# Moving half of attention's K projection into the w2 stage as a seven-product scheme

## The chip, the cores and the metric

The kernel runs on one core of one Trainium2 chip. The metric is device time in microseconds (us). A time of a kernel is the median of its runs, with the lowest and the highest in brackets. "Span" is the time from the first to the last instruction of the one execution that was profiled; it is some 2 us shorter than the device time of the same kernel (654.1 us against a median of 655.91 before).

The engines are called PE or TensorE (matmul), VectorE (DVE in the profile), ScalarE (ACT), GpSimd (POOL) and SyncE (SP, which issues nearly all DMAs here: 266 of 267 in the kernel before).

## The reference

One layernorm of x feeds two branches, whose results are added to x: a token-mixing MLP (B) and an attention with a memory over four segments (A). Only what bears on the change:

```python
# x: 2048 tokens x 1024, bf16; 32 heads of 32; N = 4 segments of L = 512 tokens
q = (xn @ wq)...; k = (xn @ wk)...; v = (xn @ wv)...      # split in heads and segments
phi = lambda t: where(t > 0, t + 1, exp(t))
M, z = 0, 0
for s in range(N):
    p = softmax(qs @ ks.T * scale + mask)                 # within the segment
    a_dot = p @ vs
    a_mem = (phi(qs) @ M) / (phi(qs) @ z + 1e-6)          # from the segments before
    outs.append(g * a_mem + (1 - g) * a_dot)
    M, z = M + phi(ks).T @ vs, z + sum(phi(ks))
attention = concat(outs) @ wo
mlp = w2.T-product of gelu(w1-product of layernorm(xn))   # over tokens; 3584 hidden
result = x + attention + mlp
```

phi(K) of the last segment is never used, so it is needed for three segments only.

## The kernel before

Three stages follow one another: w1 pairs, w2 pairs, attention.

**The seven-product stages.** A pair of output column blocks is computed as a product of 2x2 blocks with seven instead of eight block products. VectorE makes the sums of the weight blocks and the differences of the activation blocks, PE makes the seven products in a fixed order, and the results are put together while they leave PSUM. A w2 pair has 7 x 14 = 98 matmuls of 128x128 by 128x512, so 14 matmuls to a product.

```python
ORDER = (1, 6, 5, 7, 2, 4, 3)
order += [(i, p) for i in range(2, n1 + self.N_W2) for p in self.ORDER]
for i, p in order:
    ...
    self.product(pair, p)                                # PE: `depth` matmuls into one bank
    (self.after1 if i < n1 else self.after2)(pair, p)    # VectorE, ScalarE, GpSimd, DMA

def add_bank(self, pair, acc, dst, src):                 # on VectorE, "part" in the profile
    ... tensor_tensor(self.tmp[dst][:], self.bank(b), self.tmp[src][:], op=ALU.add)

def after2(self, pair, p):
    ...
    elif p == 4:
        finish("Y", 1, 0, t1); self.put_out(...)         # store to DRAM
        if i + 2 < self.N_W2:
            self.load_w2(i + 2)                          # 1.8 MB
    ...
    if i == self.N_W2 - 1:
        self.before_attention(p)                         # at p == 2: loads wo, 2 MB
```

**Attention.** It runs in 32 units, eight groups of four heads in each of four segments. Between the logits and the weighted sums, dense jobs of eight matmuls (projections q, k, v and the output product wo) fill PE. A dense job takes bank 6 or 7 in turn, and so it waits until the job before last has been copied out of that bank: K on VectorE (`kT`), q on ScalarE. In the views below, `ost` are a unit's weighted sums copied out of PSUM, `prod` and `o_s` its scaled and added output, `oT` the transpose of that, and `fin` the rows of the result.

```python
STOPS, STOPS_DVE = (1, 4, 7), (1, 4)

def dense(self, n, side=True):                # n matmuls of the waiting jobs
    while n > 0 and self.jobs:
        ...                                   # bank 6 or 7 in turn
        elif self.side and stop in stops:
            self.side.popleft()()             # hand one item of side work to VectorE here

def unit_jobs(self, u):
    jobs = [self.wo_job(*x) for x in self.wo_plan.get(u, ())]
    if m < 2 * N_SEG: jobs.append(self.v_job(m, u % 4))
    if u + 2 < N_UNIT: jobs += [self.q_job(u + 2), self.k_job(u + 2)]
    return jobs

def attention(self):
    ...                      # wo jobs of segment 2 in units [27, 28, 29, 30, 30, 31, 31, 31]
    self.load_fin(0); self.load_fin(1)
    for u in range(N_UNIT):
        even = u % 2 == 0
        if u in self.XN_AT[::4]:
            self.xn_load(xn); self.xn_load(xn + 1)        # x for the next segment: "xs"
        if u < 10:
            cuts = self.cut(total, (0, 4, 2, 4, 1, 13, 8) if even else (7, 3, 2, 4, 1, 15))
        else:
            cuts = self.cut(total, (0, 4, 2, 2, 2, 14, 8) if even else (7, 3, 2, 2, 2, 16))
        self.dense(cuts[0]); self.logits(u, 0)            # logits, then a 128x2048 exp on ScalarE
        self.dense(cuts[1], end); ...; self.weigh(u - 1, 0)
        ...
        if N_GRP <= u: self.side.append(lambda u=u: self.phi_q(u))
        if u + 1 < N_UNIT: self.side.append(lambda u=u: (self.phi_k(u + 1), self.k_transpose(u + 1)))
        if xn is not None: self.side.append(lambda c=xn: (self.xn_scale(c), self.xn_transpose(c), ...))
        self.dense(cuts[4]); self.logits(u, 1)
        if even: self.dense(cuts[5]); self.logits(u, 2)   # this exp serves both units of the pair
        self.dense(100)
```

Two units share five big exps (three in the even, two in the odd one). So the time from the first exp of an even unit to the first exp of the next even unit is the time of a pair of units, and I read all of attention by these starts.

The softmax here doesn't subtract the row's maximum and nothing guards it: scores larger than these inputs give would overflow.

## Time and profile before

Time before: 655.91 us (655.87 to 655.92, four runs).

| what | value | read from |
|---|---|---|
| span | 654.1 us | page |
| PE busy | 98% of the span | page, busy table |
| chain of waits | 92% on matmuls | page, chain |
| w2 stage up to the first big exp | 182 to 363.8 us | stretches, exps |
| pair of units with 48 dense matmuls (units 2 to 7) | 15.02 us | starts of exps |
| pair of units with 64 (units 12, 14, 20, 22) | 18.93 us | starts of exps |
| from unit 30's first exp to the end | 31.6 us | starts of exps, span |

First the page of the kernel before: busy time by engine, then the shares of the chain of waits by engine.

```profile
span 654.1 us, 11050 instructions
...
PE 642.6 (98%) x4572; PEld 303.4 (46%) x4627; DVE 422.5 (65%) x797; ACT 276.1 (42%) x297; POOL 152.9 (23%) x181
...
PE 92%; DVE 4%; issue 1%; DMA 1%; ACT 1%; SPq 0%; DVEq 0%
```

PE is the bound: nearly the whole span can be followed back through matmuls. The next view, of the same kernel, is busy time in stretches of the span. Its columns are the stretch, its length, the busy time of PE, weight loads, VectorE, ScalarE and GpSimd (with instruction counts), the granted PE clock, the DMA share and GB/s.

```profile
182.00:349.00 167.00, 167.00 (x775) 75.61 (x774) 70.34 (x89) 6.44 (x11) 34.17 (x29) 1.00 0.59 157
363.80:438.00 74.20, 72.26 (x787) 36.01 (x800) 50.57 (x120) 59.76 (x50) 27.37 (x40) 1.00 0.73 156
607.20:654.10 46.90, 43.15 (x444) 22.30 (x451) 35.38 (x68) 21.95 (x16) 14.46 (x16) 1.00 0.39 105
```

The w2 stage has room everywhere but on PE: VectorE works 70 of 167 us, ScalarE 6. That invites the change. The last two units are another matter. The timeline of ScalarE in the kernel before (start, duration, line, tiles, and in brackets the idle time before with its releaser) shows exps of which the last three begin 2.38 us apart, although each takes 1.88:

```profile
622.46 1.88 ACT L1216 ACTIVATE pT<-ps_all 128x2048 bf16<-128x2048 f32 x1 [0.66 <-PE ps_all L198]
...
625.22 1.88 ACT L1216 ACTIVATE pT<-ps_all 128x2048 bf16<-128x2048 f32 x1 [0.36 <-PE ps_all L198]
627.60 1.88 ACT L1216 ACTIVATE pT<-ps_all 128x2048 bf16<-128x2048 f32 x1 [0.50 <-PE ps_all L198]
629.98 1.88 ACT L1216 ACTIVATE pT<-ps_all 128x2048 bf16<-128x2048 f32 x1 [0.50 <-PE ps_all L198]
```

The exp needs the logits, and the logits need the banks that the exp before has read. In none of the profiled runs do two of these exps begin closer than 2.37 us, so I take this round trip of about 2.38 us as a floor, an estimate from these starts.

### The profile page before, as it was taken

Reading aid. Unit: us, or ns where it says so; the run is one execution under the profiler, and the core shown is the slowest. Engines: PE = TensorE matmul, PEld = TensorE weight load, DVE = VectorE, ACT = ScalarE, POOL = GpSimd, SP = SyncE. Lnnn points to the kernel's source line nnn. Section 1 sums busy time; section 2 is a strip of 40 time slices with the busy share of each in tenths; the row PEclk is TensorE's granted clock in tenths of the full one; section 3 lists DMA queues with packets and bytes.
Section 4 is the critical chain, followed back from the end, with each engine's and each line's share of the span. In section 5 each row is a group of like instructions: output and inputs, shape, how many; then the busy total and the mean of one; then the engine's idle time right before and its main releaser. Section 6 shows DMA issues by size and latency. Waiting matters only on the chain.

```text
span 654.1 us, 11050 instructions
## 1 busy us (share of the span) xinstructions
PE 642.6 (98%) x4572; PEld 303.4 (46%) x4627; DVE 422.5 (65%) x797; ACT 276.1 (42%) x297; POOL 152.9 (23%) x181
## 2 busy tenths in 40 slices
PE   8999999999999999999999999999999999999998
PEld 3444444444444444444444445554554455454444
DVE  6885775665644553355422376688889988867795
ACT  6642232232210000000011677886766777667760
POOL 2410000000010222022210234343243324323450
DMA  9804242242557546854386587865547754544325
GB/s 301 215 0 130 65 114 80 65 124 69 144 162 189 150 123 165 194 144 115 96 225 201 138 171 144 170 146 114 130 114 177 146 128 92 121 113 82 83 81 137
DMA packets 187258, 87.65 MB, mean 134 GB/s; under 512 B 116040, under 2 KB 174408, under 8 KB 187208
## 3 DMA queue, kind: packets, MB, share of 16 engines
q1 hardware_dynamic: 187064, 86.91, 53.0%
q8 instruction: 36, 0.59, 0.4%
q14 instruction: 14, 0.11, 0.0%
q10 hardware_dynamic: 144, 0.03, 0.0%
HBM read 67.13 MB, written 8.39 MB: 115 GB/s over the span
## 4 chain that ended last, share of the span: by engine, by line
PE 92%; DVE 4%; issue 1%; DMA 1%; ACT 1%; SPq 0%; DVEq 0%
PE ps_all L198 92%; DMA w1early<-in_B_w_dram 1%; ACT pT L1216 1%; DVE fin L1448 1%; DVE prod L1313 1%; DVE ost L1267 1%; DVE mtmp L1080 0%; DVE mtmp L1082 0%; SPq L220 0%; DVE fin L1158 0%; DVE kT L1112 0%; DVE xs L986 0%; DVE srec L1309 0%; DVE MZbf L1277 0%; DVE pqT L1082 0%
## 5 line engine op out<-in xcount | busy, mean ns | idle before, releaser
L1216 ACT ACTIVATE pT<-ps_all 128x2048 bf16<-128x2048 f32 x80 | 150.1, 1876 | 55.6 <-PE ps_all L198 55.6
L1220 POOL TENSOR_SCALAR_AFFINE_SELECT pT<-pT 128x512 bf16<-128x512 bf16 x128 | 104.1, 831 | 189.0 <-ACT pT L1216 188.8
L690 DVE TENSOR_TENSOR part<-ps_all,part 128x512 f32<-128x512 f32 x76 | 52.5, 691 | 118.9 <-PE ps_all L198 118.1
L926 POOL TENSOR_TENSOR part<-part,stg 128x512 f32<-128x512 f32 x24 | 33.0, 1404 | 263.5 <-DVE part L690 263.5
L695 ACT ACTIVATE part<-ps_all 128x512 f32<-128x512 f32 x20 | 11.9, 597 | 149.0 <-PE ps_all L198 149.0
L742 ACT ACTIVATE g<-part,b1c 128x512 f16<-128x512 f32 x36 | 26.0, 722 | 98.8 <-DVE part L690 98.8
L198 PE MATMUL ps_all<-wv,xnT 128*128 128x512 bf16 x238 | 64.6, 379 | 1.8 <-issue 0.6
L198 PE MATMUL ps_all<-wo,oT 128*128 128x512 bf16 (+2 forms) x254 | 61.0, 366 | 1.1 <-issue 0.6
L198 PE MATMUL ps_all<-xnT,wq 128*128 128x512 bf16 x248 | 61.2, 380 | 0.2
L198 PE MATMUL ps_all<-xnT,wk 128*128 128x512 bf16 x245 | 59.6, 379 | 1.5 <-issue 1.4
L1267 DVE CAST ost<-ps_all 128x396 bf16<-128x396 f32 (+2 forms) x96 | 44.5, 475 | 23.8 <-PE ps_all L198 22.3
L198 PEld LDWEIGHTS ps_all<-vA,pT 128*128 128x128 bf16 x1280 | 45.6, 96 | 20.3 <-DVE ost L1267 3.5
L198 PE MATMUL ps_all<-g,w2s 128*128 128x512 f16 x224 | 51.0, 379 | 0.0
L198 PE MATMUL ps_all<-g,sum 128*128 128x512 f16 x224 | 51.0, 379 | 0.0
L198 PE MATMUL ps_all<-gT,sum 128*128 128x512 f16 x224 | 49.7, 379 | 0.0
L198 PE MATMUL ps_all<-vA,pT 128*128 128x33 bf16 x1280 | 48.5, 177 | 0.7 <-DVE ost L1267 0.5
L198 PE MATMUL ps_all<-h,sum 128*128 128x512 f16 x192 | 45.2, 379 | 0.0
L198 PE MATMUL ps_all<-h,w1s 128*128 128x512 f16 x192 | 44.9, 379 | 0.0
L198 PE MATMUL ps_all<-hT,sum 128*128 128x512 f16 x192 | 43.6, 379 | 0.0
L198 PEld LDWEIGHTS ps_all<-xnT,wk 128*128 128x128 bf16 x256 | 23.8, 98 | 29.8 <-issue 3.2
L198 PEld LDWEIGHTS ps_all<-xnT,wq 128*128 128x128 bf16 x256 | 22.8, 97 | 26.9 <-issue 4.6
L198 PEld LDWEIGHTS ps_all<-wo,oT 128*128 128x128 bf16 x272 | 23.6, 97 | 24.5 <-issue 5.4
(99 smaller groups left out, 817.6 us busy)
## 6 DMA issues: line engine op xcount, KB each, us to landing
w2s<-in_B_w_dram SPq DMA_DIRECT2D x8, 1792.0 KB, 8.5
w1s<-in_B_w_dram SPq DMA_DIRECT2D x12, 1024.0 KB, 5.6
wq<-in_A_wq_dram SPq DMA_DIRECT2D x32, 256.0 KB, 3.4
wk<-in_A_wk_dram SPq DMA_DIRECT2D x32, 256.0 KB, 3.7
stg<-in_A_x_dram SPq DMA_DIRECT2D x16, 256.0 KB, 2.9
xs<-in_A_x_dram SPq DMA_DIRECT2D x16, 256.0 KB, 3.4
out_dram<-stg SPq DMA_DIRECT2D x16, 256.0 KB, 3.0
fin<-out_dram SPq DMA_DIRECT2D x16, 256.0 KB, 3.4
```

Source lines behind the costliest of these rows:

```text
L198: ins = self.nc.tensor.matmul(*args, **kwargs)
L690: self.fw.op("dve", lambda e: e.tensor_tensor(self.tmp[dst][:], self.bank(b), self.tmp[src][:], op=ALU.add), reads=[self.R_bank[b], self.R ...
L695: self.fw.op("act", lambda e: e.activation(self.tmp[dst][:], self.bank(b), ACT.Copy), reads=[self.R_bank[b]], writes=[self.R_tmp[dst]])
L742: self.fw.op("act", lambda e: e.activation(self.gB[f % 2][half][:, f // 2, :], src, ACT.Gelu_apprx_tanh, bias=self.b1c[:, f:f + 1], scale= ...
L926: fw.op("pool", lambda e: e.tensor_tensor(self.tmp[t][:], self.tmp[t][:], self.stg[k][:, 512 * half:512 * half + 512], op=ALU.add), reads= ...
L1216: fw.op("act", lambda e: e.activation(dst, src, ACT.Exp, scale=SCALE), reads=self.R_bank[0:4], writes=[R[v % 2][kb] for v, kb, _ in blocks ...
L1220: fw.op("pool", lambda e: e.affine_select(d, d, pattern=[[0, 4], [1, P]], compare_op=ALU.is_ge, fill=0.0, base=0, channel_multiplier=-1), ...
L1267: fw.op("dve", lambda e: e.tensor_copy(dst, src), reads=[self.R_bank[b]], writes=[self.R_ost[o][part]])
L1313: fw.op("dve", lambda e: e.tensor_tensor(self.prod[:], ost[:, :, 0:D_HEAD], rec.unsqueeze(2).to_broadcast([P, 32, D_HEAD]), op=ALU.mult), ...
L1448: fw.op("dve", lambda e: e.tensor_tensor(dst, self.ps[:, b, c0:c1], dst.bitcast(F16), op=ALU.add), reads=[self.R_bank[b], R], writes=[R])
```

## The change

Intent: K of segments 2 and 3 (half of K, 128 matmuls in attention) is computed by the same seven-product scheme in the w2 stage, where it needs 4 column pairs x 7 products x 4 matmuls = 112. One K product follows each product of w2 pairs 3 to 6. K, and phi(K) of segment 2, go to DRAM and are read back by their unit. Space and queues are rearranged for it: one w2 sum buffer instead of two, segment 0's x transposes in the last w2 pair, eight x transposes for K in w2 pairs 0 to 2, the 2 MB load of wo at the start of attention. In attention the distribution of side work ("stops") and of the wo jobs changes too. The `cuts` of the first units (how many dense matmuls stand between the logits) now hold wherever `total` is at most 26, so in the last units too, and the wo jobs from c = 9 on lose their third stop.

```diff
-        order += [(i, p) for i in range(2, n1 + self.N_W2) for p in self.ORDER]
+        for i in range(2, n1 + self.N_W2):
+            g = i - n1 - self.K_FIRST                       # K_FIRST = 3, N_KP = 4
+            for p in self.ORDER:
+                order.append((i, p))
+                if 0 <= g < self.N_KP:
+                    order.append((("k", g), p))
 ...
+    def after_k(self, pair, p):                             # cut
+        ... fw.dma(self.k_d..., self.kout[row][:], ..., is_output=True)      # K to DRAM
+        ... fw.dma(self.pk_d[v], e, ..., is_output=True)                      # phi(K) to DRAM
+    TOKENS_AT = (2, 3, 5, 6, 8, 9, 11, 12)
+    def k_prepare(self, i, p):                              # called at the end of after2
+        n = 7 * i + self.ORDER.index(p)
+        if n in self.TOKENS_AT:
+            ... self.xn_scale(c, F16); self.fw.dma(self.xnK[...], ..., transpose=True, own=True)
+        n -= 7 * (self.K_FIRST - 1)
+        if 0 <= n < 4:
+            self.differences(self.kB, self.R_kB, self.kD, self.R_kD, (n + 1,))
 ...
     def before_attention(self, p):
         elif p == 2:
             self.wo, (self.R_wo,) = take("wo", [P, N_GRP, D_MODEL], BF16)
-            fw.dma(self.wo[:], self.A_wo..., writes=[self.R_wo])
 ...
-        return [..., end, self.STOPS if c >= 9 else self.STOPS_DVE]       # wo_job, cut
+        return [..., end, True]                                          # always the second tuple
 ...
-    STOPS, STOPS_DVE = (1, 4, 7), (1, 4)
+    STOPS = ((1, 4, 7), (1, 4))
+    STOPS_FEW = ((1, 3, 5, 7), (1, 3, 5))
 ...
-            jobs += [self.q_job(u + 2), self.k_job(u + 2)]
+            jobs.append(self.q_job(u + 2))
+            if u + 2 < N_UNIT // 2:
+                jobs.append(self.k_job(u + 2))
+            else:
+                self.k_load(u + 2)
 ...
-            at = ... if s < 2 else [27, 28, 29, 30, 30, 31, 31, 31]
+            at = ... if s < 2 else [26, 27, 28, 29, 30, 30, 31, 31]
 ...
         self.load_fin(0)
         self.load_fin(1)
+        self.fw.dma(self.wo[:], self.A_wo..., writes=[self.R_wo])
         for u in range(N_UNIT):
 ...
-            if u < 10:
+            if total <= 26:
 ...
+            self.stops = self.STOPS_FEW if total <= 26 and u >= N_GRP else self.STOPS
```

## The prediction

> **What bounds the kernel now.** TensorE (PE). The chain of waits lies 92% on matmuls; the busy table has PE at 98% of 654.1 us. Busy time is modelled, so I read the weight loads in the timeline: in the w2 stage (180 to 349 us) a 14-matmul product starts every 3.02 us, 216 ns per 128x512 matmul. [...] In attention (349 to 654 us) a pair of units with 48 dense matmuls takes 15.02 us (starts of the big exps), one with 64 takes 18.9 to 19.4: 16 x 216 ns more, plus the memory products. PE is the limit there too. Only in the last four units do ScalarE's 1.88 us exps and PE wait for each other: in unit 30, with 16 dense matmuls, exps follow at 2.76, 2.38, 2.38 us instead of 3.41, 2.59, 2.81.
>
> **Removed.** 128 K matmuls from attention: 27.6 us of PE. Off PE, worth nothing directly: 16 PSUM copies on VectorE (0.69 us), 8 exps (0.62), 8 phi pairs (0.41 + 0.73).
>
> **Added.** 4 x 7 x 4 = 112 matmuls in w2 pairs 3 to 6: 24.2 us. VectorE gets some 7.5 us more per pair; it was busy 70 of 167 us there (table of stretches), ScalarE 6.4. DMA gets 8 more transposes, 8 K stores, 8 phi stores, and 16 K loads for 16 weight loads. Each has at least one product (3 us), mostly a whole unit (7.6 us) of slack against transfers of 2 to 4 us. Banks and part tiles are of the other parity, so PE should run without a hole: 27.2 us per pair instead of 21.1.
>
> **Moved.** Segment 0's transposes into the last w2 pair (21 us, need about 12); wo's 2 MB to the start of attention, used ten units later; one w2 sum buffer instead of two.
>
> **On the critical path.** 128 - 112 = 16 matmuls: -3.45 us. Against it: units 28 to 31 now have 16 dense matmuls each (before 24, 24, 16, 24). In unit 30, 8 fewer saved 1.3 us rather than 1.73, with a floor near 2.4 us between exps, so I lose about 1.5 us. Pairs 16 and 18 cost 0.4 us above their neighbours and may get it back (-0.5). New small waits: +0.5. Sum: -2.0 us (an estimate from these durations).
>
> **Predicted: 653.9 us, 651.8 to 656.6 (8 in 10). Faster by over 2%: 1%; within 2%: 98%; slower by over 2%: 1%.**
>
> **What would show each step.** (1) w2 pairs 3 to 6 at 27.2 us, no PE gap, the stage 24 us longer. (2) Unit pairs 14 to 24 at about 15.5 us. (3) Pair 28 at about 12.7 us where matmuls alone allow 11.8, ScalarE releasing PE. (4) No PE wait for xnT, wq or wk at the start of attention. (5) 16 matmuls fewer.
>
> **What would make it wrong.** PE waiting for VectorE between K products (adds late behind the 1.1 us w2 sums); K loads or phi transposes from DRAM slower than a unit; SyncE's in-order queue blocked, so weights come late; bank 6/7 evacuated too late with 24 dense matmuls per unit, so pairs 14 to 26 take 16 us or more. These cost 1 to 5 us. If all 16 matmuls count and the exps' floor doesn't bind, 652.

-3.45, +1.5, -0.5 and +0.5 make -1.95, written as -2.0, and the first of them is 16 matmuls at the 216 ns that the trace gives (3.02 us for a product of 14). Where this text calls SyncE's queue in-order, and an expectation VectorE's, the trace after shows as much: at 222.30 us one DMA held SyncE for 6.20 us, and the next was issued at 228.54; VectorE's K copy, whose matmuls PE had started by 398.44, began at 401.93, behind a scaling that had waited 8.16 us for x.

## The result, and the profile after

Time after: 667.47 us (665.60 to 668.08, four runs), against 655.91 us before. The ratio is 1.0172, with a 95% interval of 1.015 to 1.0193: slower by 1.7%, within the 2% class but 11 us outside the predicted range. Ratios are the mean time of one kernel's fast runs over that of the other's of the same rounds, so not quite the ratio of the medians quoted here.

The page after, in the lines that answer to those of before. The row PEclk was not there before; it is the granted PE clock in 40 slices, in tenths.

```profile
span 664.9 us, 11143 instructions
...
PE 643.0 (97%) x4560; PEld 303.7 (46%) x4611; DVE 440.9 (66%) x829; ACT 281.7 (42%) x305; POOL 156.0 (23%) x181
...
PEclk9999999999999999999999997999999999999999
...
PE 55%; DVE 5%; issue 3%; DMA 2%; ACT 1%; SPq 0%; DVEq 0%
```

PE's busy time is the same although it has 16 matmuls fewer; one slice ran at a lower clock; and the chain of waits goes through matmuls for 55% of the span. That last figure can't be compared with the 92% as it stands: the shares add up to 66%, because the chain, followed back from the end, breaks off at 222.30 us, at an x transpose that comes up again below.

The starts of the big exps divide the 10.8 us of added span (664.9 - 654.1). "Due" is the change in matmuls times 0.2157 us, the pace of matmuls in the w2 stage (3.02 us for the 14 of a product).

| part | before | after | change | due |
|---|---|---|---|---|
| start to unit 0's first exp | 363.80 | 389.84 | +26.04 | +24.16 (112 matmuls) |
| pair 0 | 13.99 | 20.74 | +6.75 | 0 |
| pairs 2 to 8 | 60.3 | 60.3 | 0 | 0 |
| pair 10 | 19.24 | 20.22 | +0.98 | 0 |
| pair 12 | 18.93 | 18.94 | 0 | 0 |
| pairs 14 to 24 | 114.2 | 93.4 | -20.8 | -20.7 (96) |
| pair 26 | 16.74 | 15.10 | -1.6 | -1.7 (8) |
| pair 28 | 15.24 | 12.89 | -2.35 | -3.45 (16) |
| unit 30 to the end | 31.64 | 33.46 | +1.82 | -1.7 (8) |
| sum | | | +10.8 | -3.45 |

So the intended exchange happened: pairs 14 to 24 gave back their matmuls to 0.1 us. Against it stand four losses: 6.75 us in pair 0, about 1.9 us before attention, 1.0 in pair 10, and 4.7 in units 26 to 31.

**Pair 0.** The timeline after, around unit 0 (SPq is SyncE issuing a DMA):

```profile
391.00 0.43 SPq L220 DMA_DIRECT2D wo<-in_A_wo_dram  x1
391.48 1.07 SPq L220 DMA_DIRECT2D xs<-in_A_x_dram  x2
...
401.46 0.55 DVE L1131 TENSOR_SCALAR xs<-xs,ln_mv,ln_rs 128x1024 bf16<-128x1024 bf16 x1 [8.16 <-DMA xs<-in_A_x_dram]
401.93 0.68 DVE L1259 CAST kT<-ps_all 128x512 bf16<-128x512 f32 x1
...
402.76 0.58 PE L198 MATMUL ps_all<-xnT,wq 128*128 128x512 bf16 x1 [4.14 <-DVE kT L1259]
...
406.88 1.88 ACT L1361 ACTIVATE pT<-ps_all 128x2048 bf16<-128x2048 f32 x1 [3.60 <-PE ps_all L198]
```

Read it from the bottom. The exp waits for PE; PE waits 4.14 us for a bank that VectorE's K copy has to free; the copy stands behind the scaling of x in VectorE's order; and that scaling waits 8.16 us for an x load that was issued just behind wo. The view of DMA issues between 385 and 405 us of the same kernel (size, and us from issue to landing) says how long these loads took:

```profile
wo<-in_A_wo_dram SPq DMA_DIRECT2D x1, 2048.0 KB, 9.8
xs<-in_A_x_dram SPq DMA_DIRECT2D x3, 256.0 KB, 10.0
```

Over the whole kernel before, the same view has for an x load:

```profile
xs<-in_A_x_dram SPq DMA_DIRECT2D x16, 256.0 KB, 3.4
```

So the x loads issued behind the 2 MB of wo took 10.0 us to land, about as long as wo itself with 9.8, where 3.4 is the median before. That their place behind wo is the cause is tested in experiments 1 to 3.

What comes after the wait is the second part. The table of stretches after:

```profile
395.00:400.00 5.00, 3.62 (x29) 1.57 (x28) 0.00 (x0) 3.57 (x2) 2.04 (x4) 1.00 1.00 344
400.00:405.00 5.00, 2.24 (x24) 1.16 (x24) 2.38 (x5) 0.63 (x1) 0.20 (x1) 0.68 0.72 172
405.00:410.00 5.00, 4.64 (x38) 2.05 (x35) 2.72 (x8) 2.37 (x2) 1.18 (x2) 0.64 0.70 169
```

The last two means, 0.68 and 0.64, come of a clock that was halved for a time: asked in slices of 1 us, the trace has it that the granted clock is 0.50 from 402 to 408 us and 1.00 again from 409 (0.89 in the slice before 402, 0.70 in that after 408), so it was low for some 6.8 us, from about 401.8 to 408.6. PE had stood idle since 398.6, and worked again from 402.76. So the wait of 4.14 us and the low clock after it cost 6.75.

**Before attention.** The timeline after, in w2 pair 2:

```profile
221.79 0.44 SPq L220 DMA_DIRECT2D w2s<-in_B_w_dram  x1
...
222.30 6.20 SPq L220 DMA_TRANSPOSE xnK<-xs  x1
...
231.57 1.23 DVE L664 TENSOR_TENSOR kD<-xnK,xnK 128x2048 f16<-128x2048 f16 x1 [7.30 <-issue]
...
232.71 0.68 DVE L690 TENSOR_TENSOR part<-ps_all,part 128x512 f32<-128x512 f32 x1
...
233.45 2.71 PEld L198 LDWEIGHTS ps_all<-g,sum 128*128 128x128 f16 x14 [2.39 <-DVE part L690]
```

The same pattern: the last x transpose for K stands behind 1.8 MB of w2 in the queue; VectorE's difference of x blocks (`kD`) waits for it; the copy-out of a bank (`part`) waits behind the difference; and PE's weight loads stand idle 2.39 us. The trace names no releaser for the wait of `kD` ("issue"). That it is the transpose is inferred: the slowest of the eight took 9.0 us from issue to landing (median 4.9), which from 222.30 ends 0.3 us before `kD` starts. Experiment 4 tests it.

**Pair 10.** With the changed stops, VectorE has an add and the phi of K before it gets to the K copy and the `ost` copies that PE needs. Timeline after:

```profile
471.76 0.73 DVE L1464 TENSOR_TENSOR o_s<-prod 128x512 bf16<-128x512 bf16 x1
...
472.74 0.69 DVE L1227 SCALAR_TENSOR_TENSOR mtmp<-kT,mtmp 128x512 bf16<-128x512 bf16 x1
...
473.34 0.68 DVE L1259 CAST kT<-ps_all 128x512 bf16<-128x512 f32 x1
...
473.94 1.04 DVE L1412 CAST ost<-ps_all 128x396 bf16<-128x396 f32 x2
...
474.56 0.57 PE L198 MATMUL ps_all<-vA,pT 128*128 128x33 bf16 x16 [1.12 <-DVE ost L1412]
```

These are readings of a trace. The experiments ask whether they are causes.

### The profile page after: what moved, and what is told of

It is laid out like the page before. It is cut to its first block, busy times and chain, and to the rows that moved or that the text cites. A ratio compares the mean times of both kernels' runs of the same rounds, so it can differ in the third digit from the quotient of the medians.

```text
span 664.9 us, 11143 instructions
## 1 busy us (share of the span) xinstructions
PE 643.0 (97%) x4560; PEld 303.7 (46%) x4611; DVE 440.9 (66%) x829; ACT 281.7 (42%) x305; POOL 156.0 (23%) x181
## 4 chain that ended last, share of the span: by engine, by line
PE 55%; DVE 5%; issue 3%; DMA 2%; ACT 1%; SPq 0%; DVEq 0%
PE ps_all L198 55%; DMA xs<-in_A_x_dram 1%; DVE prod L1458 1%; DVE ost L1412 1%; ACT pT L1361 1%; DVE fin L1604 1%; SPq L220 0%; DMA oT<-o_s 0%; DVE fin L1304 0%; DMA xnK<-xs 0%; DVE o_s L1464 0%; DVE srec L1454 0%; DVE mtmp L1225 0%; DVE kT L1259 0%; DVE srec L1455 0%
## 5 line engine op out<-in xcount | busy, mean ns | idle before, releaser
L1365 POOL TENSOR_SCALAR_AFFINE_SELECT pT<-pT 128x512 bf16<-128x512 bf16 x128 | 107.4, 856 | 168.9 <-ACT pT L1361 168.7
L690 DVE TENSOR_TENSOR part<-ps_all,part 128x512 f32<-128x512 f32 x84 | 57.7, 690 | 105.4 <-PE ps_all L198 85.0
L198 PE MATMUL ps_all<-wo,oT 128*128 128x512 bf16 (+2 forms) x256 | 63.0, 366 | 1.8 <-DMA oT<-o_s 0.8
L198 PE MATMUL ps_all<-wv,xnT 128*128 128x512 bf16 x242 | 62.9, 380 | 0.6 <-issue 0.2
L695 ACT ACTIVATE part<-ps_all 128x512 f32<-128x512 f32 x24 | 14.0, 596 | 103.3 <-PE ps_all L198 69.2
L1458 DVE TENSOR_TENSOR prod<-ost,srec 128x1024 bf16<-128x1024 bf16 x24 | 36.8, 1533 | 0.0
L198 PE MATMUL ps_all<-qT,kT 32*128 32x384 bf16 (+3 forms) x512 | 31.9, 303 | 4.0 <-ACT pT L1361 1.9
L198 PEld LDWEIGHTS ps_all<-g,sum 128*128 128x128 f16 x224 | 21.9, 98 | 28.6 <-DVE part L690 2.6
```

The lines of the kernel that those rows point to most:

```text
L198: ins = self.nc.tensor.matmul(*args, **kwargs)
L690: self.fw.op("dve", lambda e: e.tensor_tensor(self.tmp[dst][:], self.bank(b), self.tmp[src][:], op=ALU.add), reads=[self.R_bank[b], self.R ...
L695: self.fw.op("act", lambda e: e.activation(self.tmp[dst][:], self.bank(b), ACT.Copy), reads=[self.R_bank[b]], writes=[self.R_tmp[dst]])
L1365: fw.op("pool", lambda e: e.affine_select(d, d, pattern=[[0, 4], [1, P]], compare_op=ALU.is_ge, fill=0.0, base=0, channel_multiplier=-1), ...
L1458: fw.op("dve", lambda e: e.tensor_tensor(self.prod[:], ost[:, :, 0:D_HEAD], rec.unsqueeze(2).to_broadcast([P, 32, D_HEAD]), op=ALU.mult), ...
```

## The experiments

All kernels gave the reference's result. Each was compared with the kernel before, run on the same chip in the same call: 655.77 us in the first call, 655.93 in the second, 655.74 in the third and fourth, 655.69 in the fifth. The granted clock of the profiled runs is 0.995 to 1.0.

Main theory: the loss is a matter of order, in the DMA queue and in VectorE's program, and not of the added work. The rival for pair 0 was bandwidth: that 2 MB more in the first units is too much wherever it stands.

### 1. wo before unit 4

```diff
-        self.fw.dma(self.wo[:], ...)          # before the loop over units
         for u in range(N_UNIT):
+            if u == 4:
+                self.fw.dma(self.wo[:], ...)
```

> The changed kernel, with one edit: the 2 MB load of wo is issued before unit 4 instead of before unit 0 (first use stays unit 10). Theory A (the moved wo load stands in front of the x loads of unit 0; VectorE's in-order queue then waits 8.2 us for x, PE waits for VectorE 4.1 us, and PE's clock drops for some 7 us): the first pair of units takes about 14.0 us as before instead of 20.7, mean clock 1.00, and the time falls by 6 to 7.5 us to about 660.5 us. Rival B (the K scheme itself, its part tiles or its K stores at the start of attention, makes that stall): first pair stays near 20 us, time stays 666 to 668.

Measured: 660.28 us (659.89 to 662.3), ratio 1.0072. Pair 0 is back at 13.99 us. About 7 of the 11.6 us were the place of one load.

This run had the same hole in w2 pair 2 as the changed kernel (2.50 us on the weight loads), and after it the clock fell. Its stretches:

```profile
231.00:234.00 3.00, 0.99 (x6) 0.26 (x4) 2.11 (x3) 0.00 (x0) 0.00 (x0) 1.00 0.49 129
234.00:238.50 4.50, 4.50 (x15) 1.71 (x14) 2.07 (x2) 0.00 (x0) 0.00 (x0) 0.62 0.23 87
```

In the changed kernel itself the hole of 2.39 us left the clock at 1.00. The lower clock is why the first exp of number 1's profiled run began at 391.8 us, not at 389.8 (4.5 us at 0.62 are 1.7 us lost); that run was also the slowest of its kernel, at 662.3 us, and the median is 2 us below it. Why the clock fell here and not there stays open: no run separates the 0.1 us of difference from anything else.

### 2. The kernel before, with only wo moved

```diff
 # before.py
-            fw.dma(self.wo[:], ...)           # in the last w2 pair
 ...
         self.load_fin(1)
+        self.fw.dma(self.wo[:], ...)
```

> The kernel before with only the wo load moved to the place that the change gives it; no K scheme. Theory A: the same stall appears without the K scheme, first pair of units about 20 us instead of 14.0, time 655.9 + 6 to 8 = about 662.5 us, granted clock under 1. Rival B: the time stays within 1 us of 655.9.

Measured: 662.37 us (662.04 to 662.6), ratio 1.0098. Pair 0 took 20.57 us in place of 13.99. Its timeline has the same chain, with none of the K work present:

```profile
364.80 0.43 SPq L220 DMA_DIRECT2D wo<-in_A_wo_dram  x1
365.27 1.07 SPq L220 DMA_DIRECT2D xs<-in_A_x_dram  x2
...
375.59 0.55 DVE L986 TENSOR_SCALAR xs<-xs,ln_mv,ln_rs 128x1024 bf16<-128x1024 bf16 x1 [8.49 <-DMA xs<-in_A_x_dram]
...
376.88 0.59 PE L198 MATMUL ps_all<-xnT,wq 128*128 128x512 bf16 x1 [4.46 <-DVE kT L1111]
```

One moved line costs 6.6 us by itself. Taken out of the changed kernel it gave 7.2, put into the kernel before it costs 6.6: that is as direct as a cause can be shown.

### 3. wo in unit 0, but behind the two x loads

```diff
             if u in self.XN_AT[::4]:
                 self.xn_load(xn)
                 self.xn_load(xn + 1)
+            if u == 0:
+                self.fw.dma(self.wo[:], ...)
```

> The changed kernel with wo issued still in unit 0, but just after the two x loads rather than just before them. Tells the order in the queue from the bandwidth that 2 MB take. If it is the order (theory A): the wait of VectorE for x falls from 8.2 to under 1 us, first pair of units 14 to 15 us, time near 660.5 to 661.5 us. If it is the 2 MB as such (rival C, any load in that stretch is slowed): the first pair stays over 18 us and the time over 664 us.

Measured: 659.99 us (659.92 to 660.91), ratio 1.0064; pair 0 is 13.99 us. Its timeline:

```profile
391.06 0.91 SPq L220 DMA_DIRECT2D xs<-in_A_x_dram  x2
392.02 0.43 SPq L220 DMA_DIRECT2D wo<-in_A_wo_dram  x1
...
395.22 0.55 DVE L1131 TENSOR_SCALAR xs<-xs,ln_mv,ln_rs 128x1024 bf16<-128x1024 bf16 x1 [1.85 <-DMA xs<-in_A_x_dram]
```

VectorE waits 1.85 us for x (under 1 was expected), and pair 0 loses nothing by it. The 2 MB move in the same microseconds, but a place later in the queue. Bandwidth, the rival, falls; order in the queue stands.

### 4. Also the w2 reload behind the transposes

```diff
 # on top of 1: in after2
         elif p == 4:
             finish("Y", 1, 0, t1); self.put_out(...)
-            if i + 2 < self.N_W2:
-                self.load_w2(i + 2)
 ...
         self.k_prepare(i, p)
+        if p == 4 and i + 2 < self.N_W2:
+            self.load_w2(i + 2)
```

> As wo_unit4, and also the reload of w2 in the fourth-product step (p = 4) is issued after the x transposes of that step instead of before them. Theory A2 (the last of the eight x transposes for K queues behind a 1.8 MB w2 load; VectorE's differences wait 7.3 us for it, PE 2.4 us for VectorE): the PE hole of 2.4 us in w2 pair 2 goes, and the time is 2.2 to 2.6 us under wo_unit4, about 658 us. Rival: the transposes or their waits are slow by themselves, then the hole stays over 1.5 us and the gain is under 0.7 us.

Measured: 658.21 us (657.99 to 658.35), ratio 1.0034. Its timeline shows the transpose in front and the difference six microseconds earlier:

```profile
222.10 1.30 SPq L220 DMA_TRANSPOSE xnK<-xs  x1
...
223.46 0.57 SPq L220 DMA_DIRECT2D w2s<-in_B_w_dram  x1
...
225.56 1.22 DVE L664 TENSOR_TENSOR kD<-xnK,xnK 128x2048 f16<-128x2048 f16 x1 [1.20 <-issue]
```

The hole is gone, and the first exp begins at 387.85 us, 24.05 after that of the kernel before where 24.16 are due. The K products as such cost their matmuls and nothing more.

### 5. The few stops only from unit 14

```diff
-            self.stops = self.STOPS_FEW if total <= 26 and u >= N_GRP else self.STOPS
+            self.stops = self.STOPS_FEW if total <= 26 and u >= 14 else self.STOPS
```

> Base: wo_unit4_tr (658.2). One edit: the denser stop pattern, at which VectorE's side work is put between the matmuls of a job, is used from unit 14 on and not in units 8 and 9. Theory: in unit 9 it puts the o_s add and the phi of K (2 us) ahead of the kT copy and of the ost copies that PE waits for; without it unit pair 10 falls from 20.2 to 19.2 us, the time to about 657.2. Rival: pair 10 is slower for another reason (product placement, wo arriving), then it stays at 20.2 and the time at 658.2.

Measured: 656.83 us (656.26 to 657.28), ratio 1.0014. Pair 10 is back at 19.24 us, as before. The median fell by 1.4, of which this pair explains 1.0.

### 6 to 8. The last units: the wo plan

In all three, segment 2's eight wo jobs are spread otherwise over units 26 to 31. Experiment 6 is number 4 with the plan of before, 7 is number 5 with the plan of before, 8 is number 5 with more jobs kept for unit 30.

```diff
-            at = ... else [26, 27, 28, 29, 30, 30, 31, 31]
+            at = ... else [27, 28, 29, 30, 30, 31, 31, 31]      # 6 and 7
+            at = ... else [28, 29, 30, 30, 30, 31, 31, 31]      # 8
```

> Base: wo_unit4_tr (658.2). One edit: the wo products of segment 2 are spread as in the kernel before (units 27, 28, 29, 30, 30, 31, 31, 31), so that unit 31 has 24 dense matmuls again and unit 26 has 16. Theory: the stretch from the first exp of unit 30 to the end, 33.3 us in the base and 31.6 before, pays for an oT transpose that comes late behind a load of fin, and for exps that PE has no work to cover. With 8 matmuls more there (+1.73 us of PE) it would still be under 34.2 us, and pair 26 loses 8 matmuls (-1.2 to -1.7 us): time 657.2 to 658.2. Rival: the tail is plain PE work, then the change moves time from pair 26 to the tail one to one and the time stays within 0.2 us of 658.2.

Measured: 657.92 us (657.47 to 658.25), ratio 1.003.

> Both edits above on wo_unit4_tr. If they are independent: the sum of the two gains, about 656.7 us (0.5 to 2 us under wo_unit4_tr).

Measured: 656.57 us (656.46 to 656.89), ratio 1.0012.

> few_from14 with the segment 2 wo products still later: units 28, 29, 30, 30, 30, 31, 31, 31, so units 26 to 29 have 16 dense matmuls each and 30 and 31 have 24. If the starved exps in the units of 16 are what is lost (each costs 0.5 to 0.7 us above its PE time), this has as many starved units as the plan of before and ends within 0.5 us of few_plan; if the end of the kernel alone matters it is 0.5 to 1 us faster than few_plan.

Measured: 656.62 us (656.52 to 656.76), ratio 1.0011.

The plan is worth 0.3 us at most. It shifts time between pairs: with number 8, pair 26 falls to 13.12 us and pair 28 rises to 13.36, and the end takes its part. No arrangement of the same jobs recovered what is missing in units 26 to 31.

### 9 and 10. Waits at the end

SyncE ends the kernel with one wait for each output store. The 16 new stores of K and phi(K) have been read back long before, so these waits can be dropped without a race.

```diff
 # on top of 7
         for t in self.out_toks:
-            sp.wait_ge(t.sem, t.val)
+            if t not in self.read_back:
+                sp.wait_ge(t.sem, t.val)
```

> Base: few_plan (656.6). One edit: SyncE no longer waits at the end for the 16 stores of K and of phi to DRAM, which the kernel has itself read back long before. Theory: after the last output DMA is issued, SyncE works through one semaphore wait per 61 ns, 28 of them and a pause of 0.4 us in few_plan, 20 in the kernel before; its output data land at 652.9 us of a 654.7 us span. Without the waits the end comes 0.5 to 0.9 us sooner: 655.7 to 656.1. Rival: the end waits for the landing of the output, then nothing changes (656.6).

Measured: 656.02 us (655.88 to 656.14), ratio 1.0004, against 1.0012 for number 7.

> The kernel before without the end waits for the 16 stores of partial results that it reads back itself. A control: there the output lands at 653.2 of 654.1 us, and the last waits end at 653.6, so at most some 0.4 us can be had: 655.4 to 655.9.

Measured, as a control on the kernel before, with the 16 waits for its own stores dropped: 655.83 us (655.63 to 656.37), ratio 1.0003. It gains nothing. So the gain of number 9, 0.4 to 0.55 us by medians, lies within overlapping intervals and isn't shown to be one.

### 11. VectorE's side work in the last units split

```diff
-            while end and self.side:
+            while end and len(self.side) > 3:
                 self.side.popleft()()
 ...
                 self.weigh(u - 1, 1)
+            while end and self.side:
+                self.side.popleft()()
```

> Base: few_plan (656.6). One edit: in the last four units VectorE's side work is emptied before the second part of weigh only as far as phi of q; the products and adds of the unit before come after the first ost copies. Theory: in units 28 to 31 the 1.7 us product and 0.7 us add stand in front of the ost copy that PE waits for (0.6 us in unit 30, whose first exp gap is 3.7 us instead of 2.8). Without that the time falls 0.5 to 1.2 us, to 655.4 to 656.1. Rival: the gap is exps alone: no change beyond 0.2 us.

Measured: 656.34 us (656.26 to 656.94), ratio 1.0011. A miss: the order of instructions at unit 30 did not change in the trace, since the side items had been handed out at stops before; the first gap between exps there stayed at 3.73 us. It says nothing for or against the theory it was made for.

### 12. All repairs together

> All of it together: few_plan, late_flush, no end waits for K, phi and partial stores. If the gains add up: 656.6 - 0.9 - 0.5 - 0.8 = about 654.4 us, that is 1.5 us under the kernel before; if they overlap, 655.3.

Measured: 655.93 us (655.62 to 655.97), ratio 1.0001, interval 0.9985 to 1.0018. With numbers 4, 7, 9 and 11 and the end waits for the older stores dropped too, the change is level with the kernel before; neither of the expected figures came. The 16 saved matmuls (3.45 us) are still missing. By the exps they are missing in units 26 to 31: with the plan of before, 32 matmuls less are due there, 6.9 us, and 3.8 us came (59.8 us from pair 26's first exp to the end, against 63.6).

### 13 to 15. Fewer products moved

If the last units are too poor in dense matmuls to use the saving, moving less should lose nothing. Kernels 13 and 14 move three of the four column pairs (groups 6 and 7 of segments 2 and 3 keep their K in attention), 15 moves two. Of the 16 saved matmuls, 12 and 8 are left. They stand on the repairs of number 12, without number 11, which had changed no order at unit 30.

```diff
-    N_KP, K_FIRST = N_GRP // 2, 3
+    N_KP, K_FIRST = 3, 3                      # 13, 14; 2 in 15
+    def own_k(self, u):
+        return u < N_UNIT // 2 or u % N_GRP >= 2 * self.N_KP
 ...
-            if u + 2 < N_UNIT // 2:
+            if self.own_k(u + 2):
                 jobs.append(self.k_job(u + 2))
```

> Base: end_waits without the end waits for the partial stores as well (about 656.0). One size changed: three of the four pairs of K column groups by the seven-product scheme (groups 0 to 5), groups 6 and 7 of segments 2 and 3 stay matmuls in attention, in units 20, 21, 28 and 29. PE saves 12 matmuls (2.6 us) instead of 16 (3.45). Theory (the gain is lost in the starved late units): unit pair 28 goes back to 15.2 us with 48 matmuls, the last stretch from unit 30 to the end from 33.6 to about 31.6 us as before, only pair 26 keeps its loss of 0.9 us; the time is 655.8 - 2.6 + 0.9 = about 654.1 us, so fewer saved matmuls make it faster. Rival (the interleaving and the way through DRAM cost it): a quarter of the saving and of the cost goes, the time stays at 655.9 to 656.1.

Measured: 655.45 us (655.37 to 658.64), ratio 1.0007.

> As three, with the segment 2 wo products as in the changed kernel (units 26, 27, 28, 29, 30, 30, 31, 31): units 26 to 29 have 24 dense matmuls each, 30 and 31 have 16. Theory: pair 26 no longer starves (15.1 us), but unit 31 has 8 fewer to cover its exp and the late oT transpose; the time is within 0.7 us of three, 654.1 to 654.8.

Measured, with the wo plan of the change: 656.09 us (655.17 to 656.67), ratio 1.0000. Here pair 6 took 16.92 us in place of 15.02.

> As three with two pairs (groups 0 to 3): K of groups 4 to 7 stays in attention, in units 18 to 21 and 26 to 29. PE saves 8 matmuls (1.73 us). Theory: all of it counts since no unit from 26 on loses a matmul: w2 stage +12.1 us, attention -13.8 us, time 655.8 - 1.7 = about 654.1 us, no slower than three. Rival: half of the saving and half of the cost, 655.8 to 656.0.

Measured: 655.44 us (655.22 to 656.88), ratio 0.9999.

Half the saved matmuls gone, and the time is the same. Numbers 15, 13 and 12 differ in the last units only in how much of K was moved, so they can be read as a series, from pair 26's first exp to the end: 63.9 us with no matmul fewer than before, 61.45 with 16 fewer, 59.8 with 32 fewer. The first 16 brought 2.5 us of the 3.45 due, the next 16 only 1.65. This agrees with the theory: the fewer dense matmuls are left there, the less their removal gives.

It doesn't explain all of the loss, though. Number 15 has as many matmuls there as the kernel before, and still took 0.3 us more (63.9 against 63.6). From unit 30 on it took 0.6 us more, in spite of the dropped end waits: unit 30's second exp comes 3.27 us after the first, where it was 2.76 before. That part isn't want of matmuls, and number 18 below shows the same 3.28 without the few stops. The new cuts put one more wo matmul (0.22 us) before that exp; no run has put the old cuts back, so the cause of this part is open.

The expected 654.1 us did not come in numbers 13 and 15, because small new holes ate the rest: 1.05 us on PE's weight loads at 335 us in number 13, 0.8 us in pair 6 in number 15.

### 16 to 18. The last units without the few stops

One rival was left for units 26 to 31: not the lack of matmuls, but the few stops, which the change had switched on there. These kernels have wo behind the x loads of unit 0 (as number 3), the few stops only in units 14 to 25, the plan and the dropped end waits of number 12, and four, three and two column pairs. They don't restore the stops of before altogether: the wo jobs from c = 9 on, which are all the dense work of units 30 and 31, had three stops before and have two here.

```diff
-            self.stops = self.STOPS_FEW if total <= 26 and u >= 14 else self.STOPS
+            self.stops = self.STOPS_FEW if total <= 26 and 14 <= u < 26 else self.STOPS
```

> All four column pairs of K moved, with every repair found so far: wo loaded in unit 0 after its two x loads, the w2 reload after the x transposes, the few stops only in units 14 to 25 (so the last six units have the stops of before), the wo plan of before, no end waits for stores that the kernel reads back. Theory starved (the last units pay because 16 fewer matmuls leave exp and VectorE as the bound, whatever the stops): no better than the same kernel with wo before unit 4 and few stops to the end, 655.9 us, so 655.5 to 656.2. Rival stops (the order of VectorE's side work in the last six units is what holds them): the tail from unit 30 falls from 33.5 to about 32, and the time to 653.8 to 654.8.

Measured: 657.12 us (655.78 to 658.13), ratio 1.002, interval 1.0007 to 1.0032.

> As four_xs, with three column pairs moved (groups 6 and 7 of segments 2 and 3 keep their K in attention). Starved: the late units are less bound, 16 matmuls more; small holes decide: pair 6 exact again at 15.0, time 654.6 to 655.3. Rival stops: about the same as four_xs, 654 to 654.8.

Measured: 656.49 us (655.82 to 656.72), ratio 1.0011.

> As four_xs, with two column pairs moved. Both theories: +12.2 before attention, -13.9 in pairs 14 to 24, pair 6 back at 15.0 because wo no longer stands before unit 4: 0.8 us less than the same kernel with wo before unit 4, about 654.4 to 654.8 (before: 655.8). If it stays at 655.4, the loss in pair 6 was not the place of wo.

Measured: 656.43 us (656.14 to 657.12), ratio 1.0015.

All three lie above what either theory expected. The rival as it was put falls: without the few stops the tail from unit 30 did not shrink to 32 us but took 33.7 in number 16, and pair 28 is 12.88 us, as with them. But the test is not clean. All three kernels have a wait of PE for the transposed output of unit 30, which numbers 12, 13 and 15 do not have (the changed kernel had one too, of 1.29 us on the weight loads), and neither has the kernel before, whose wo jobs had the third stop. In number 16:

```profile
638.86 0.42 DVE L1466 TENSOR_TENSOR o_s<-prod 128x512 bf16<-128x512 bf16 x1
...
639.91 1.21 SPq L221 DMA_TRANSPOSE oT<-o_s  x1
...
643.01 2.33 PE L199 MATMUL ps_all<-wo,oT 128*128 128x512 bf16 x10 [1.10 <-DMA oT<-o_s]
```

In number 12 the same add began at 637.60 us and the transpose was issued at 638.36, before the loads of partial results and not after one; in the kernel before, the add also comes ahead of the sum of a result row (`fin`), at 636.60 us. So an order of VectorE's side work does cost up to 1.1 us here, and the lost third stop is the likely cause; no run tried it alone. Read as a series, from pair 26's first exp to the end, numbers 18, 17 and 16 took 64.5, 62.2 and 60.8 us: again 2.3 and then 1.4 us for 16 matmuls each, and 0.9 us lost with no matmul fewer.

Number 18 answered the other question: pair 6 is back at 15.02 us, so its loss in number 15 went away with the place of wo. The time did not follow, since this run had 0.9 us more before attention (PE waits of 0.69 and 1.19 us on the weight loads in the w2 stage where number 15 has 0.39 and 0.46, in code that is the same up to the end of that stage) and 0.6 us more in the tail. Holes of up to a microsecond in the w2 stage thus differ between executions of the same instructions, and a version that beats the kernel before by more than that was not found.

What bounds units 26 to 31 can be read in number 16; it is a reading, not an experiment. Stretches of pair 28, number 16 first:

```profile
608.10:621.00 12.90, 11.78 (x153) 5.91 (x152) 11.10 (x22) 11.48 (x10) 6.33 (x9) 1.00 0.37 104
```

and the kernel before:

```profile
607.20:622.50 15.30, 15.09 (x166) 7.29 (x169) 12.05 (x24) 11.48 (x10) 6.07 (x8) 1.00 0.36 87
```

Before, PE is busy 15.09 of 15.30 us. Without 16 matmuls PE has 11.78 us of work, VectorE 11.10 and ScalarE 11.48, and the pair takes 12.9: three engines of nearly the same load that pass work to each other in order. Number 16's timeline at unit 30 shows how the remaining microsecond arises:

```profile
620.53 1.68 DVE L1460 TENSOR_TENSOR prod<-ost,srec 128x1024 bf16<-128x1024 bf16 x1
...
622.25 0.74 DVE L1466 TENSOR_TENSOR o_s<-prod 128x512 bf16<-128x512 bf16 x1
...
622.91 1.03 DVE L1414 CAST ost<-ps_all 128x396 bf16<-128x396 f32 x2
...
623.52 0.57 PE L199 MATMUL ps_all<-vA,pT 128*128 128x33 bf16 x16 [0.58 <-DVE ost L1414]
...
624.76 1.88 ACT L1363 ACTIVATE pT<-ps_all 128x2048 bf16<-128x2048 f32 x1 [1.34 <-PE ps_all L199]
```

VectorE is still on unit 29's results when unit 30's first exp runs at 621.02; PE waits for its copies, and the next exp comes 3.74 us after the last, where it took 2.76 before (and 3.28 in number 18, with as many matmuls as before: about half of that microsecond is not for want of matmuls). PE work that is removed here in good part only brings the next limit forward.

## Why the prediction was wrong

Predicted were 653.9 us, in a range of 651.8 to 656.6; measured were 667.47. The class, within 2%, held; the range did not.

What was right:

- PE is the bound, and matmuls count at 0.2157 us (96 fewer took 20.8 us off pairs 14 to 24, where 20.7 are due). Step (2), pairs 14 to 24 at about 15.5 us: they took 15.25 to 15.81. Step (3), pair 28 at about 12.7: it took 12.89, with the exps 2.38 us apart.
- Step (1), the K products at their matmuls: with the queue order mended, 24.05 us (number 4). In the changed kernel itself the "no PE gap" failed, in pair 2 and not among the products.
- The 0.4 us of pairs 16 and 18 came back (19.36 to 15.70, which is 0.2 more than due in each).

What failed, with the predicted words:

1. "Moved. ... wo's 2 MB to the start of attention, used ten units later": the prediction gave this no cost, because wo's own use is far away. It asked when the moved transfer is needed, and not what is issued behind it. The x loads behind it were needed by VectorE within a few microseconds: its scaling of x waited 8.16 us, the K copy stood behind that, and PE waited 4.14 us for the copy. Measured: 6.75 us in pair 0, of which 4.14 are waiting and the rest is mostly the reduced clock, 0.50 for some 6.8 us (experiments 1, 2, 3). Step (4), "No PE wait for xnT, wq or wk at the start of attention", named the right place to look. "SyncE's in-order queue blocked, so weights come late" was among the risks at 1 to 5 us, but with the wrong victims.
2. "Each has at least one product (3 us), mostly a whole unit (7.6 us) of slack against transfers of 2 to 4 us": the transposes were costed at 2 to 4 us each as though alone. The last one, behind the w2 reload, was issued at 222.30 and its reader started at 231.57. Measured: 1.9 us net before attention (experiment 4 gives back 2.0).
3. "New small waits: +0.5": pair 10 alone had 1.0 (experiment 5). The order of VectorE's side work was read from the diff as a detail.
4. "I lose about 1.5 us" in units 28 to 31: the right mechanism with too small a size. Due were 6.9 us from 32 matmuls in units 26 to 31, and 4.7 of them were lost in the changed kernel, 3.1 with all repairs (experiment 12). Of these 3.1, numbers 12, 13 and 15 put 2.8 down to the want of matmuls; 0.3 was lost with no matmul fewer, to edits that the prediction did not cost at all. The prediction took only the floor between exps, and not VectorE, whose load in pair 28 had come close to PE's; that this is what the 2.8 us are is read from the stretches, not tested.

The sum closes: -3.45 due, +6.75, +1.9, +1.0, +4.7 makes +10.9 us, against 10.8 of span. Most of the miss is step 1; without it the kernel took 660 us (experiments 1 and 3), and without steps 2 and 3 as well 656.83 (number 5).

What is open: where the last 0.5 to 1 us of the repaired versions goes from run to run in the w2 stage; whether the 16 dropped end waits are worth anything; and whether another order of VectorE's work in units 26 to 31 would do better, as number 11 failed to change it, and as no run put back the cuts of before or the third stop of the wo jobs there. Open too is why the 128x1024 product on VectorE (`prod`), with the same shape, had a median of 1218 ns before and 1652 ns after. In these two timelines it took 1.65 to 1.69 us in 19 of the 20 cases that start while a select on GpSimd (`pT`) is already running, and 1.22 or 1.23 us in all others, also where a select starts during it; no run tried the one without the other. What the single w2 sum buffer costs was not tried alone; number 4, at 24.1 us for 112 matmuls, leaves it no room to cost.

## What to carry to other kernels

When a large transfer is moved, look at what is issued behind it in the same queue and at which engine waits for that in order; its own deadline says nothing about them. Here 256 KB loads behind 2 MB took 10.0 us to land in place of 3.4. A hole on TensorE is to be costed with the clock that follows it: here one of 4.14 us cost 6.75, with the granted clock at 0.50 for some 6.8 us, while one of 2.39 us left it at 1.00. And before moving matmuls out of a stage, add up the load of the other engines there: in number 16, 3.45 us of matmuls less made pair 28 only 2.36 us shorter, with PE at 11.78 us of work, VectorE at 11.10 and ScalarE at 11.48. So take the saving from stages where PE alone is full and leave the rest. (Numbers 13 to 15 did so; here it kept them level with the kernel before and gained nothing clear of the noise.)
